# A second head's sums leave their bank by one copy and two transfers

## The chip, the cores and the metric

One core of a Trainium2 chip runs the whole program. The metric is device time in microseconds (us) for one execution. The kernel before takes 528.98 us (median of 3 runs, 528.67 to 529.69).

## The reference, cut to what matters

Three stages follow each other: attention with rotary embedding (2 batches, 8 heads, 576 tokens, 64 wide), a dense feed-forward layer with softplus (1152 tokens, 512 to 2048 to 512), and a mixture of 8 experts of which each token takes one. The change lies in the first stage:

```python
q_rot, k_rot = (rotate(q), rotate(k))
scores = scale * np.matmul(q_rot, k_rot.transpose(0, 1, 3, 2))
scores = scores - np.max(scores, axis=-1, keepdims=True)
attn = np.exp(scores)
attn = attn / (np.sum(attn, axis=-1, keepdims=True) + 1e-09)
attn_out = np.matmul(attn, v)
x = attn_out.transpose(0, 2, 1, 3).reshape(B * S, H * D)
x = x @ w_in            # feed-forward, softplus, w_out, then the experts
```

## The kernel before, in words

Precision is kept by splitting numbers into a high and a low part and adding two or three matmuls, so nearly each PSUM bank is read twice: ScalarE copies the high part (`acopy`, L71), VectorE subtracts it from the bank to get the low part (`vsub`, L74).

**Pairs and slots.** The 16 heads are worked on as 8 pairs (pair 0 to 3 of batch 0, 4 to 7 of batch 1). One loop of slots (the loop over `s`) sets the order of the work on all engines by hand: 9 slots to a pair, 72 in all, and 17 more that mix the last pairs with the feed-forward layer. A slot of pair m computes one 128-row block of scores (`scores`, L526 on TensorE), its maximum (L543 on VectorE) and, in the next slot, its exponentials (L544 on ScalarE). Between these stand the transposes of an earlier pair's exponentials (`turn`, L314) and their products with v (`av`, L612). What is put off to a later slot goes through `later(n, f)`: f is called at the end of the n-th slot from now, and things of one slot in the order in which they were put in.

**The bank of sums.** `av` adds the products of one head of a pair in bank 7 of PSUM (`acc`, 128 rows x 512 tokens). Half of the rows hold the high part of v's product, the other half the low part: head 0 has its high part in rows 0 to 63, head 1 in rows 64 to 127. When a head is through, `fin(m, h)` takes the bank away, and the next head's first `av` (L612, stationary tile from `g`) can only write bank 7 after that. Head 0 of a pair is done at slot 8, head 1 at slot 3 of a period, one and two periods after the pair's own scores.

**Where the sums go.** `xp` (a ring of two buffers, part of the tile the trace calls `g`) is to hold the high parts of both heads, `x_sw` (one buffer, part of the tile `fa`) the low parts, in the same rows as the high ones. So rows have to change halves. Head 0: one copy of all 128 rows into `xp`, and a DMA from `xp`'s lower half to `x_sw`'s upper half (L674). Head 1: two copies by ScalarE of 64 rows each, one to `xp`, one with a change of rows to `x_sw` (L676 and L677, both through L71). Then `finish(m)` on GpSimd (POOL) adds `x_sw` (L691), multiplies by the reciprocals (L687) and splits into the feed-forward layer's input (L68, L81), one step to a slot, from the second slot after on. The last pair (m = 7) goes another way on VectorE.

**What else stands on these queues.** SP issues nearly all DMAs, in program order. In each period it brings the next pair's keys and queries to their places: `kqt` duplicates halves (L335), inserts the last tokens' keys (L350 to L355), brings the low part of the queries (L365), and `load` fetches raw inputs (L233). A score block of the next pair waits for L335 and L365. POOL does the rotary embedding of the pair after next (`rotary`, L264, four steps over four slots), low parts of v (L81), the spreading of reciprocals (L68) and `finish`.

**Scratch.** `y_tl[b]` (128 x 512, part of tile `g`) gathers the last 64 tokens of batch b over its four pairs (`av_tails`), and `x_tails(b)` transposes it after them (slot 65 for batch 0).

Of the kernel before, what the change touches and what calls it, by code (L numbers as in the profile page):

```python
# [20 lines left out]
def kernel(  # L21
# [15 lines left out]
    nc = tc.nc  # L37
# [6 lines left out]
    NP = H // 2  # L44
# [9 lines left out]
    NPR = NH // 2  # L54
# [15 lines left out]
    def acopy(o, i):  # L70
        nc.scalar.activation(out=o, in_=i, func=ACTF.Copy)  # L71
# [116 lines left out]
    y_tl = [vm.take(512), r_tmp.bufs[0]]  # L188
    x_sw = xm[:, 4608:5120]
# [10 lines left out]
    def later(n, fn, start=False):  # L200

        queue.setdefault((now[0] + n, start), []).append(fn)
# [458 lines left out]
    def fin(m, h):  # L661

        r, o = slice(64 * h, 64 * h + 64), slice(64 - 64 * h, 128 - 64 * h)
        if h == 0:
            xps[m] = r_xp.next()
        xp = xps[m]
        acc = pp[:, 7, :]
        if m == NPR - 1:
            tmp = r_tmp.next()
            acopy(tmp[r], acc[o])  # L670
            return lambda: nc.vector.tensor_tensor(out=xp[r], in0=acc[r], in1=tmp[r], op=ALU.add)
        if h == 0:
            acopy(xp, acc)
            nc.sync.dma_start(out=x_sw[r], in_=xp[o])  # L674
        else:
            acopy(xp[r], acc[r])  # L676
            acopy(x_sw[r], acc[o])  # L677
        return None

    def finish(m):  # L680
        b, p = divmod(m, NP)
        last = m == NPR - 1
        eng = nc.vector if last else nc.gpsimd
        xp = xps[m]
        xh, xl = (xt[b][a][:, p, 0:512] for a in range(2))
        steps = [
            lambda: eng.tensor_tensor(out=xp, in0=xp, in1=rsb[m], op=ALU.mult),  # L687
            lambda: (acopy if last else pcopy)(xh, xp),
            lambda: (vsub if last else psub)(xl, xp, xh.bitcast(F32)),
        ]  # L690
        return steps if last else [lambda: eng.tensor_tensor(out=xp, in0=xp, in1=x_sw, op=ALU.add)] + steps  # L691
# [680 lines left out]
    for s in range(NSL + 17):  # L1372
        m, i = divmod(s, 9)
        ma = m - 1 if 4 <= i <= 8 else m - 2
# [7 lines left out]
        if ending:  # L1382
            add = fin(ma, i == 3)
# [29 lines left out]
            add()  # L1413
        if ending and i == 3:
            for n, f in enumerate(finish(ma)):
                later(n + 2, f)
        if extra:
            extra[1]()

# [423 lines left out]
```

## Time and profile before

| | before |
|---|---|
| median of the runs | 528.98 us |
| profiled execution | 529.54 us |
| its span, first to last instruction | 527.8 us |
| TensorE busy in the span | 502.5 us (95%) |
| ScalarE busy | 313.5 us (59%) |
| GpSimd busy | 286.3 us (54%) |
| granted TensorE clock, mean | 0.994 |

The attention's slots lie between about 20 and 190 us of the span; ScalarE, VectorE and GpSimd are much busier there than in the rest. A row of the timeline gives the start and the length of a run of like instructions, and in brackets the idle time of its engine just before it with the name of what ended it. PE rows are matmuls, PEld rows the loading of their stationary tiles, SPq rows the issuing of DMAs (how long SP is held by it, not the transfer).

### The profile page before, as it was taken

Reading aid. Unit: us, or ns where it says so; the run is one execution under the profiler, and the core shown is the slowest. Engines: PE = TensorE matmul, PEld = TensorE weight load, DVE = VectorE, ACT = ScalarE, POOL = GpSimd, SP = SyncE. Lnnn points to the kernel's source line nnn. Section 1 sums busy time; section 2 is a strip of 40 time slices with the busy share of each in tenths; the row PEclk is TensorE's granted clock in tenths of the full one; section 3 lists DMA queues with packets and bytes.
Section 4 is the critical chain, followed back from the end, with each engine's and each line's share of the span. In section 5 each row is a group of like instructions: output and inputs, shape, how many; then the busy total and the mean of one; then the engine's idle time right before and its main releaser. Section 6 shows DMA issues by size and latency. Waiting matters only on the chain. (4 is left out here: it accounts for less than half of the span.)

```text
span 527.8 us, 9308 instructions
## 1 busy us (share of the span) xinstructions
PE 502.5 (95%) x3184; PEld 448.0 (85%) x3184; DVE 351.4 (67%) x766; ACT 313.5 (59%) x662; POOL 286.3 (54%) x308
## 2 busy tenths in 40 slices
PE   8688999999989999999999999999999999999995
PEld 7577888889878999999998788888888989898794
DVE  7867887878899789999898222367656347156220
ACT  5578898999987666655976333345443255345321
POOL 1698889688435655655448655466775535300001
PEclk9989999999999999999999999999999999999998
DMA  7156646545562334544430000522221467500000
GB/s 175 41 136 168 160 120 154 155 115 129 118 185 66 107 120 127 158 149 146 148 122 2 20 22 21 156 67 80 70 95 43 144 264 257 199 9 21 20 6 34
DMA packets 45096, 57.09 MB, mean 108 GB/s; under 512 B 17112, under 2 KB 31448, under 8 KB 45040
## 3 DMA queue, kind: packets, MB, share of 16 engines
q1 hardware_dynamic: 41904, 48.76, 32.4%
q0 software_dynamic: 2704, 7.25, 4.1%
q8 instruction: 27, 0.44, 0.4%
q10 hardware_dynamic: 432, 0.41, 0.2%
q14 instruction: 29, 0.24, 0.2%
HBM read 40.17 MB, written 5.16 MB: 86 GB/s over the span
## 5 line engine op out<-in xcount | busy, mean ns | idle before, releaser
L845 PE MATMUL pp<-rm,parts 128*128 128x512 f32 x432 | 105.5, 397 | 0.4 <-POOL parts L81 0.4
L803 PE MATMUL pp<-xb,rm 128*128 128x288 f32 x768 | 104.4, 295 | 1.1 <-DVE g L820 0.8
L803 PEld LDWEIGHTS pp<-xb,rm 128*128 128x128 f32 x768 | 102.0, 188 | 1.9 <-issue 1.0
L845 PEld LDWEIGHTS pp<-rm,parts 128*128 128x128 f32 x432 | 79.2, 188 | 16.6 <-POOL parts L81 0.9
L314 PE MATMUL pp<-ct,g 128*128 128x128 f32 x388 | 59.0, 274 | 4.3 <-ACT g L71 1.3
L74 DVE TENSOR_TENSOR rm<-pp,rm 128x512 fp32r<-128x512 f32 (+3 forms) x79 | 52.5, 669 | 15.2 <-ACT rm L71 13.8
L544 ACT ACTIVATE g<-pp,negm 128x576 f32<-128x576 f32 x72 | 53.3, 740 | 7.9 <-DVE negm L543 7.5
L314 PEld LDWEIGHTS pp<-ct,g 128*128 128x128 f32 x388 | 46.8, 140 | 13.0 <-DVE rm L74 2.0
L543 DVE TENSOR_REDUCE negm<-pp 128x1 f32<-128x576 f32 x72 | 54.0, 749 | 5.5 <-PE pp L526 5.5
L526 PE MATMUL pp<-rm 128*128 128x288 f32 x216 | 47.6, 329 | 6.3 <-DMA rm<-rm 2.8
L81 POOL TENSOR_TENSOR rm<-fa,rm 128x512 fp32r<-128x512 f32 x34 | 46.3, 1362 | 13.3 <-ACT rm L71 11.0
L1079 PE MATMUL pp<-wa,parts 128*128 128x512 f32 x216 | 51.1, 392 | 0.0
L71 ACT ACTIVATE rm<-pp 128x512 fp32r<-128x512 f32 (+3 forms) x73 | 42.2, 582 | 12.2 <-PE pp L314 7.8
L68 POOL TENSOR_SCALAR rm<-fa 128x512 fp32r<-128x512 f32 x27 | 17.9, 664 | 56.2 <-DVE fa L731 51.4
L1079 PEld LDWEIGHTS pp<-wa,parts 128*128 128x128 f32 x216 | 39.9, 188 | 7.9
L1222 PE MATMUL pp<-wa,wa 128*128 128x256 f32 x320 | 46.3, 283 | 0.0
L81 POOL TENSOR_TENSOR parts<-g,parts 128x512 fp32r<-128x512 f32 (+1 forms) x30 | 36.2, 1224 | 16.7 <-ACT parts L71 16.6
L1222 PEld LDWEIGHTS pp<-wa,wa 128*128 128x128 f32 x320 | 43.0, 192 | 0.2
L526 PEld LDWEIGHTS pp<-rm 128*128 128x128 f32 x216 | 32.5, 194 | 11.8 <-ACT g L544 6.6
L612 PE MATMUL pp<-rm,rm 128*128 128x512 f32 x128 | 41.0, 413 | 0.0
L728 DVE SCALAR_TENSOR_TENSOR fa<-fa 128x512 int32<-128x512 int32 x32 | 40.5, 1265 | 0.8
L264 POOL TENSOR_TENSOR fa<-fa,g 128x512 f32<-128x512 f32 (+1 forms) x30 | 37.2, 1257 | 2.9 <-DMA fa<-in_q_dram 2.0
(219 smaller groups left out, 907.0 us busy)
## 6 DMA issues: line engine op xcount, KB each, us to landing
fa<-in_moe_w_in_dram SPq DMA_DIRECT2D x16, 512.0 KB, 3.9
fa<-in_moe_w_out_dram SPq DMA_DIRECT2D x16, 512.0 KB, 3.5
fa<-in_moe_w_dram SPq DMA_DIRECT2D x16, 512.0 KB, 6.1
rm<-rm SPq DMA_DIRECT2D x56, 128.0 KB, 2.4
ydram<-yst SPq DMA_DIRECT2D x9, 264.0 KB, 2.1
fa<-in_k_dram SPq DMA_DIRECT2D x8, 256.0 KB, 2.9
yst<-in_v_dram SPq DMA_DIRECT2D x8, 256.0 KB, 3.4
st<-in_moe_w_dram POOLq DMA_DIRECT2D x4, 512.0 KB, 8.0
```

What stands on the lines that cost most here:

```text
L71: nc.scalar.activation(out=o, in_=i, func=ACTF.Copy)
L74: nc.vector.tensor_tensor(out=o, in0=a, in1=b, op=ALU.subtract)
L81: nc.gpsimd.tensor_tensor(out=o, in0=a, in1=b, op=ALU.subtract)
L314: nc.tensor.matmul(out=bank[0:a.shape[1], i * 128:(i + 1) * 128], lhsT=a, rhs=ident, is_transpose=True, start=True, stop=True,)
L526: nc.tensor.matmul(out=ps[:, o:o + HS], lhsT=st, rhs=mv[:, k0 + o:k0 + o + HS], start=(x == 0), stop=(x == len(terms) - 1),)
L543: nc.vector.tensor_reduce(out=negm[:, col:col + 1], in_=ps, axis=AX.X, op=ALU.max, negate=True)
L544: return lambda: nc.scalar.activation(out=pr, in_=ps, func=ACTF.Exp, bias=negm[:, col:col + 1], accum_out=sums[:, col:col + 1])
L612: nc.tensor.matmul(out=pp[:, 7, :], lhsT=w, rhs=mv, start=(j == 0 and n == 0), stop=(j == 3 and n == len(terms) - 1))
L803: nc.tensor.matmul(out=hp[:, f, :], lhsT=wv[:, c * 128:(c + 1) * 128], rhs=xt[b][xi][:, c, f * HS:(f + 1) * HS], start=(n_mm == 0), stop=( ...
L845: nc.tensor.matmul(out=ybank(t), lhsT=ghl[gi][:, qd, c, :], rhs=wo[4 * qd + c][wi], start=(qd == 0 and c == 0 and gi == 0 and wi == 0), st ...
L1079: nc.tensor.matmul(out=pp[:, bank, :], lhsT=hid[a][i], rhs=wl[1][i], start=(i == 0 and a == 0 and wl is W.hi), stop=(i == K2F - 1 and a == 1),
L1222: nc.tensor.matmul(out=hp, lhsT=wl[0][2 * c + i // 4][:, i % 4 * 128:i % 4 * 128 + 128], rhs=mem[xi][c], start=(c == 0 and xi == "hi" and ...
```

## The change

For head 1 of pairs 0, 1, 2, 3, 5 and 6, ScalarE no longer makes two copies of 64 rows; it makes one copy of all 128 rows into `both`, which is the `y_tl` of the batch that does not need it at that time, and SP issues two transfers of 64 x 512 numbers, one to `x_sw` and one to `xp`. Pair 4 keeps its two copies (both `y_tl` are in use then), and pair 7 is not touched. The steps of `finish` start one slot later for all pairs but the last.

```diff
         if h == 0:
             acopy(xp, acc)
             nc.sync.dma_start(out=x_sw[r], in_=xp[o])
-        else:
+        elif m == NP:
             acopy(xp[r], acc[r])
             acopy(x_sw[r], acc[o])
+        else:
+
+            both = y_tl[0 if m > NP else 1]
+            acopy(both, acc)
+            nc.sync.dma_start(out=x_sw[r], in_=both[o])
+            nc.sync.dma_start(out=xp[r], in_=both[r])
         return None
...
         if ending and i == 3:
             for n, f in enumerate(finish(ma)):
-                later(n + 2, f)
+                later(n + (2 if ma == NPR - 1 else 3), f)
```

On SP, in the period in which pair 1's second head ends, this stood before (`rm` are the tiles of keys and queries, `fa` holds raw inputs, rotated inputs and `x_sw`, `g_92` holds `xp`):

```order
L355 DMA rm<-rm 128x64
L335 DMA rm<-rm 64x512 x2
L233 DMA fa<-in_q_dram 128x2x256
L335 DMA rm<-rm 64x512 x4
L365 DMA rm<-fa 64x512 x2
L389 DMA rm<-rm 64x4x64 x4
L674 DMA fa<-g_92 64x512
```

and this stands now (`g_92` holds `both` and `xp`):

```order
L355 DMA rm<-rm 128x64
L335 DMA rm<-rm 64x512 x2
L682 DMA fa<-g_92 64x512
L683 DMA g_92<-g_92 64x512
L233 DMA fa<-in_q_dram 128x2x256
L335 DMA rm<-rm 64x512 x4
L365 DMA rm<-fa 64x512 x2
L389 DMA rm<-rm 64x4x64 x4
L674 DMA fa<-g_92 64x512
```

The two new transfers stand between the keys' transfers and the queries' transfers of the pair after; the same holds in the periods of pairs 0, 2 and 3.

On POOL, in the same period, from the spreading of reciprocals on (`rc`), this stood before (`rm_89` is v, `xb_85` and `xb_86` the feed-forward input's high and low part):

```order
L68 TENSOR_SCALAR g_92<-rc 128x512
L264 TENSOR_TENSOR fa<-fa,g_92 128x512
L691 TENSOR_TENSOR g_92<-g_92,fa 128x512
L264 TENSOR_TENSOR fa<-fa,g_92 128x512
L687 TENSOR_TENSOR g_92<-g_92,fa 128x512
L264 TENSOR_TENSOR fa<-fa 128x2x4x32
L81 TENSOR_TENSOR rm_89<-yst,rm_89 128x4x64
L68 TENSOR_SCALAR g_92<-g_92 128x64
L68 TENSOR_SCALAR xb_85<-g_92 128x512
L264 TENSOR_TENSOR fa<-fa 128x2x4x32
L81 TENSOR_TENSOR rm_89<-yst,rm_89 128x4x64
L81 TENSOR_TENSOR xb_86<-g_92,xb_85 128x512
```

and this stands now (the addition is L697 there, the multiplication L693):

```order
L68 TENSOR_SCALAR g_92<-rc 128x512
L264 TENSOR_TENSOR fa<-fa,g_92 128x512 x2
L697 TENSOR_TENSOR g_92<-g_92,fa 128x512
L264 TENSOR_TENSOR fa<-fa 128x2x4x32
L81 TENSOR_TENSOR rm_89<-yst,rm_89 128x4x64
L68 TENSOR_SCALAR g_92<-g_92 128x64
L693 TENSOR_TENSOR g_92<-g_92,fa 128x512
L264 TENSOR_TENSOR fa<-fa 128x2x4x32
L81 TENSOR_TENSOR rm_89<-yst,rm_89 128x4x64
L68 TENSOR_SCALAR xb_85<-g_92 128x512
L264 TENSOR_TENSOR fa<-fa,g_92 128x512
L81 TENSOR_TENSOR xb_86<-g_92,xb_85 128x512
```

The addition moved behind the second step of the rotation, and the last split behind the first step of the next rotation; the amount of work is the same.

## Rows read from the trace of the kernel before

**Rows 1.** The page: busy us, share of the span, instructions.
```profile
PE 502.5 (95%) x3184; PEld 448.0 (85%) x3184; DVE 351.4 (67%) x766; ACT 313.5 (59%) x662; POOL 286.3 (54%) x308
```

**Rows 2.** Waits, 55 to 180 us: who waited for whom, total, times, longest.
```profile
PEld pp L612 <- ACT fa L71: 2.9, 5, 0.7
...
PE pp L612 <- ACT fa L71: 2.3, 6, 0.5
```

**Rows 3.** Timeline of ACT, 59 to 70 us: start, length, engine, line, tiles, shape.
```profile
59.40 0.59 ACT L71 ACTIVATE g<-pp 64x512 f32<-64x512 f32 x1
60.01 0.59 ACT L71 ACTIVATE fa<-pp 64x512 f32<-64x512 f32 x1
...
69.35 0.60 ACT L71 ACTIVATE g<-pp 128x512 f32<-128x512 f32 x1
```

**Rows 4.** Timeline of PE, 60 to 108 us; in brackets the idle time.
```profile
60.65 0.73 PE L612 MATMUL pp<-g 128*128 128x512 f32 x2 [0.43 <-ACT fa L71]
...
70.31 0.43 PE L526 MATMUL pp<-rm,xd 128*128 128x288 f32 x2
...
89.96 0.53 PE L526 MATMUL pp<-rm 128*128 128x288 f32 x2 [0.47 <-DMA rm<-fa]
...
100.48 0.60 PE L314 MATMUL pp<-ct,fa 128*128 128x128 f32 x4
...
107.98 0.43 PE L526 MATMUL pp<-rm,xd 128*128 128x288 f32 x2
```

**Rows 5.** Timeline of SP's issuing, 55 to 125 us.
```profile
63.10 0.58 SPq L233 DMA_DIRECT2D fa<-in_q_dram  x1
64.22 2.51 SPq L335 DMA_DIRECT2D rm<-rm  x4
66.83 1.18 SPq L365 DMA_DIRECT2D xd<-fa  x2
...
74.20 1.28 SPq L386 DMA_DIRECT2D rm<-rm  x2
...
81.52 2.25 SPq L335 DMA_DIRECT2D rm<-rm  x2
83.81 0.59 SPq L233 DMA_DIRECT2D fa<-in_q_dram  x1
84.49 2.99 SPq L335 DMA_DIRECT2D rm<-rm  x4
87.58 1.18 SPq L365 DMA_DIRECT2D rm<-fa  x2
...
91.53 0.55 SPq L674 DMA_DIRECT2D fa<-g  x1
...
100.74 0.58 SPq L233 DMA_DIRECT2D fa<-in_q_dram  x1
101.90 3.08 SPq L335 DMA_DIRECT2D rm<-rm  x4
105.08 1.19 SPq L365 DMA_DIRECT2D xd<-fa  x2
...
118.64 0.58 SPq L233 DMA_DIRECT2D fa<-in_q_dram  x1
120.36 2.38 SPq L335 DMA_DIRECT2D rm<-rm  x4
```

**Rows 6.** DMA issues: tiles, queue, count, KB each, median us to landing.
```profile
fa<-g SPq DMA_DIRECT2D x7, 128.0 KB, 4.4
rm<-fa SPq DMA_DIRECT2D x6, 128.0 KB, 2.3
```

**Rows 7.** Timeline of PEld, 150 to 156 us.
```profile
155.62 0.30 PEld L526 LDWEIGHTS pp<-rm 128*128 128x128 f32 x2 [0.31 <-ACT g L544]
```

**Rows 8.** Timeline of POOL, 79 to 92 us.
```profile
79.40 1.29 POOL L691 TENSOR_TENSOR g<-g,fa 128x512 f32<-128x512 f32 x1 [1.54 <-ACT fa L71]
...
90.78 1.44 POOL L264 TENSOR_TENSOR fa<-fa 128x256 f32<-128x256 f32 x2
```

## The prediction

> **What bounds the kernel now.** I read the busy line of the page first. TensorE is busy for 502.5 of the 527.8 us of the span [rows 1], so only something that removes or adds idle time on TensorE can move the end; ScalarE, at 59%, matters only where TensorE waits for it. So the second view is that of the waits over the attention's slots. It names the line that this change touches: TensorE's products with v (L612) wait for ScalarE's copy to `fa`, which is the second head's copy to `x_sw`. By TensorE's matmul rows this is 2.3 us over six of the seven copies, by the rows of the weight loads 2.9 us over five [rows 2]. The two count the same waits from different ends: the end of a matmul is modelled, the load of the next stationary tile is not hidden after a wait. Third, the timelines show why. ScalarE makes the two 64-row copies one after the other, 0.59 us each; the second ends at 60.60, and TensorE's next head starts at 60.65 after 0.43 us of idle time [rows 3, 4]. Fourth, I read SP's timeline in the same stretches, since that is the queue on which the change puts something.
>
> **What it removes.** A 128-row copy takes 0.60 us, as the first heads' copies show, and a 64-row copy 0.59 [rows 3]: what a copy takes hangs on its columns, not on its rows. So one copy in place of two frees the bank and ScalarE 0.6 us earlier, six times, and the first five of the six waits go. (The sixth of the waits in the view is pair 4's, which is left as it is; pair 6's copy has none.) The mean wait is 2.3 / 6 = 0.38 by the matmuls and 2.9 / 5 = 0.58 by the loads [rows 2]. I take 0.5, so five of them are 2.5 us, with 1.9 and 2.9 as ends. ScalarE being 0.6 us ahead also helps the exponentials just behind; the one place where the next score block visibly waits for them is in pair 5's period, 0.31 us [rows 7], and I take 0.3 for it. Together 2.8 us gained, if nothing is given back.
>
> **What it adds.** Twelve transfers of 128 KB, two in each of six periods. The issue of one holds SP for 0.55 us (L674, same shape), two of the next larger sort for 1.18 (L365) [rows 5]: I take 1.2 us for a pair of them. The ends are 1.1 (two at 0.55) and 2.25 (the dearest pair in these rows, L335 at 81.52) [rows 5]. From issue to landing a lone 128 KB transfer of this form needs 2.3 us, and one from `g` to `fa` had a median of 4.4 [rows 6].
>
> The price hangs on what stands behind them on SP: the raw queries' load, the duplication of the next pair's queries (L335) and their low parts (L365), for which the next pair's first score block waits. I follow TensorE's lead over the kernel before through the periods (minus is earlier).
> - Pair 0. The copy gives -0.5. SP is done with the load at 63.68 and had to wait until 64.22 for ScalarE, so 0.54 of the 1.2 us are free and L365 goes from 66.83 to 67.5 [rows 5]. It lands 2.3 later at 69.8 [rows 6]. The score block that reads it started at 70.31 [rows 4] and would now start at 69.8: just in time, but four transfers more or less at once may be slower. I take 0.2 as lost: -0.3.
> - Pair 1. The copy gives another -0.5. But here SP issues without a pause from 74.20, where it is released by ScalarE, to the end of L365 at 88.76, and TensorE already waits 0.47 us for this very transfer at 89.96 [rows 4, 5]. SP's chain starts 0.3 earlier and is 1.2 longer: L365 at 88.5, landed at 90.8. TensorE stands at +0.85. What two copies gave is gone, and more.
> - Pair 2. -0.5 makes +0.35. SP's run begins with ScalarE's work and so 0.85 later; its pause of 0.58 before 101.90 is used up: L365 goes from 105.08 to 106.6 and lands at 108.9, where TensorE read it at 107.98 [rows 4, 5]. +0.9.
> - Pair 3. -0.5 makes +0.4. SP has 1.14 us of pause between the load (ends 119.22) and the duplication at 120.36 [rows 5], enough for the two issues, and no wait for a transfer stands in TensorE's rows there. +0.4.
> - Pair 5. -0.5 and the 0.3 from above make -0.4. No queries are moved any more. Pair 6: no wait before, none after.
>
> So about 2.4 of the 2.8 us are given back and -0.4 is left. Against its own execution (529.54: span 527.8, 1.74 around it) that is 529.1; against the median of the runs, which is 0.56 lower, **528.6 us**.
>
> The Trainium skill speaks against my largest term. The page "DMA: Bandwidth & Descriptors", section "Issuing engines are not separate DMA queues", says that the sequencer time it takes to start a DMA is usually small beside the DMA itself. By that rule two more issues would not count, and the result would be that of the second case below. The rows differ from it here: 0.59 us of issue stand against 2.3 to landing, but SP issues without a pause from 74.20 to 88.76 [rows 5], and at 89.96 it is the end of this row of issues that TensorE waits for.
>
> **The later finish on POOL.** The addition waited 1.54 us for ScalarE's copy [rows 8]. Now it waits for two transfers. In pair 1's period these are issued from about 83.5 on and land by 86.6, so POOL, in order, stands for some 7 us instead, with two steps of one rotation and all of the next behind it. That next rotation ended at 92.2 [rows 8] and would end near 98; its reader, TensorE's transposes of the rotated inputs, comes at 100.48 [rows 4]. I cost this at nothing, with these 2 to 3 us as its cover. If the transfers need 4.4 us instead of 2.3, the cover falls below 1 us.
>
> **The rivals.**
> - *Hidden issues (the full gain).* SP's 1.2 us are swallowed, for instance because its long issues (0.75 mean in the four at 84.49, 1.1 in the two at 81.52 [rows 5]) are pauses that would happen anyway and overlap. For it: SP does pause in pairs 0, 2 and 3. Against it: the 0.47 at 89.96. Time: 528.98 - 2.8 = 526.2, with 1.9 alone 527.1; I say 526.6.
> - *POOL held by the transfers (slower).* The addition stands in order before the rotations. From a landing of about 5 us after the issue on, the transposes at 100.48 and their like in the next two periods wait. L674's median of 4.4 [rows 6] speaks for it; that it is issued just ahead of larger loads, as the new ones are too, explains it. With a landing of 5.5 to 6.5 us TensorE waits about 1 us in each of three periods beside the forecast's -0.4: 528.98 - 0.4 + 3 x 0.9 = 531.3; with two of three 530.4.
> - *Dear issues (slower or same).* A pair of issues takes the upper end, 2.25. Then pairs 1 and 2 end 1 us later each, against which pair 3's pause gives some back: +1.0 on top of the forecast, 529.6.
> - *The bank is not what holds L612.* Then TensorE waits at the same place for the exponentials and only the 1.2 us on SP remain: about 529.5. Against it: start at 60.65, 50 ns after the copy's end.
>
> **How the numbers follow.** Forecast 0.45 (own range 527.9 to 529.6), hidden issues 0.32, POOL held 0.13, dear issues 0.06, another holder of the bank 0.04. A measurement of this kernel can tell about 0.2%, 1.1 us, from no change, so faster means under 527.9 and slower over 530.0. Faster: 0.29 of the second case, 0.05 of the first, 0.34. Slower: 0.12 from POOL, 0.02 each from the last two, 0.04 from the forecast's upper tail, 0.20. The rest, 0.46, is the same. The range for 8 times in 10 is 526.4 to 530.4: from nearly all of the gain to POOL held in two of three periods.
>
> **What would show it.** Right: in the profile after, L612's waits for ScalarE's copy shrink to pair 4's one; SP's rows show the two issues between L335 and the load, about 1.2 us; the wait of TensorE for `rm` from `fa` (0.47 at 89.96) grows to 1.5 to 2.5 us at the first block of pair 4, and a smaller one appears at the block of pair 5. POOL's addition waits for a DMA and no longer for ScalarE, without anyone waiting for POOL's rotations. Wrong: no wait for L335 or L365 grows (then it is the full gain), L314 waits for POOL's L264 (then the slower rival), or L612 waits at the same place for something else.

## The result and the profile after

The changed kernel takes **534.42 us** (median of 6 runs, 533.19 to 539.89), the kernel before in the same session 529.12 (6 runs, 527.74 to 530.58). The ratio is 1.0116, 95% interval 1.007 to 1.0161: slower, where 528.6 with a range up to 530.4 was forecast. The profiled execution took 534.74, with a span of 533.1 and a granted clock of 0.996; that of before had 529.54, 527.8 and 0.994. Between 58 and 131 us the granted clock is 1.00 in both, so the clock is not where the 5.3 us of span went.

The busy line of the page after answers to [rows 1]:

```profile
PE 502.7 (94%) x3184; PEld 448.2 (84%) x3184; DVE 355.9 (67%) x766; ACT 308.0 (58%) x656; POOL 286.5 (54%) x308
```

TensorE is busy as long as before (502.7 against 502.5), so the whole loss is idle time. ScalarE lost six instructions and 5.5 us of work, and VectorE gained 4.5 us of busy time with the same 766 instructions. Of these 4.5 us, 4.1 are in the first step of the reciprocals (L550), whose 16 instructions have a mean of 435 ns instead of 181: five of them lie beside operations of GpSimd here, one of these (at 37.93 us) before anything of the change has run. Some 3 us behind each of the other four, TensorE's transposes wait for VectorE (L314 for L74): 1.6 us in four waits, where it was 0.7 in one.

The view of waits, 55 to 190 us, TensorE's matmul rows (who waited for whom, total, times, longest), answers to [rows 2]:

```profile
PE pp L526 <- DMA rm<-rm: 3.0, 2, 1.9
PE pp L526 <- ACT g L544: 2.0, 3, 1.4
...
PE pp L612 <- DVE rm L74: 0.7, 2, 0.4
PE pp L526 <- DMA xd<-fa: 0.7, 2, 0.4
PE pp L612 <- ACT fa L71: 0.4, 1, 0.4
PE pp L612 <- POOL g L81: 0.3, 1, 0.3
```

The wait that the change aims at went from 2.3 us in six to 0.4 in one, pair 4's, as forecast. In its place stands L526, the score block that opens the next pair: 3.0 us for `rm` from `rm`. That is L335, the duplication of the queries; L365, on which the prediction counted, ends a second, shorter wait of the same blocks. Two waits for VectorE (L612 <- DVE) were in nobody's sum.

Two rows of the timeline before that are needed for the comparison:

```profile
59.43 0.79 PE L526 MATMUL pp<-rm 128*128 128x288 f32 x4
...
126.04 0.78 PE L526 MATMUL pp<-rm 128*128 128x288 f32 x4
```

TensorE's timeline after, first the row ahead of the first copy, then those that answer to [rows 4]:

```profile
60.05 0.80 PE L526 MATMUL pp<-rm 128*128 128x288 f32 x4
60.68 0.62 PE L612 MATMUL pp<-g 128*128 128x512 f32 x2
...
71.06 0.50 PE L526 MATMUL pp<-rm 128*128 128x288 f32 x2 [1.09 <-DMA rm<-rm]
71.91 0.54 PE L526 MATMUL pp<-rm,xd 128*128 128x288 f32 x2 [0.35 <-DMA xd<-fa]
...
92.18 0.50 PE L526 MATMUL pp<-rm 128*128 128x288 f32 x2 [1.90 <-DMA rm<-rm]
92.87 0.54 PE L526 MATMUL pp<-rm 128*128 128x288 f32 x2 [0.19 <-DMA rm<-fa]
...
111.33 0.50 PE L526 MATMUL pp<-rm 128*128 128x288 f32 x2 [1.35 <-ACT g L544]
112.18 0.54 PE L526 MATMUL pp<-rm,xd 128*128 128x288 f32 x2 [0.36 <-DMA xd<-fa]
...
130.64 1.16 PE L526 MATMUL pp<-rm 128*128 128x288 f32 x4 [0.32 <-issue]
```

The block at 60.05 stood at 59.43 in the kernel before, so this execution came 0.62 late out of the start, before anything of the change had run. I take that off. The first product after the copy (60.68 against 60.65 before) has no wait any more and is 0.6 us early. Then the lead turns round: +1.0 at 71.91, +2.3 at 92.87, +3.6 at 112.18, against -0.3, +0.85 and +0.9 in the prediction. (The row at 111.33 names ScalarE as the last to release it: exponentials that run from 110.50 to 111.23. The same ones of pair 0's period run from 70.50 to 71.23, and the block there starts at 71.06, before their end. So the block does not need them, and L335 is left, whose issues end at 109.3; 2.9 us to landing, the median below, fit.)

SP's issuing in pairs 0, 1 and 2 (start, length, line, tiles, count) answers to [rows 5]:

```profile
62.48 2.10 SPq L335 DMA_DIRECT2D rm<-rm  x2
64.67 0.55 SPq L682 DMA_DIRECT2D fa<-g  x1
65.27 0.59 SPq L683 DMA_DIRECT2D g<-g  x1
65.91 0.58 SPq L233 DMA_DIRECT2D fa<-in_q_dram  x1
66.59 2.40 SPq L335 DMA_DIRECT2D rm<-rm  x4
69.09 1.18 SPq L365 DMA_DIRECT2D xd<-fa  x2
...
85.14 1.77 SPq L683 DMA_DIRECT2D g<-g  x1
...
87.64 2.38 SPq L335 DMA_DIRECT2D rm<-rm  x4
90.12 1.19 SPq L365 DMA_DIRECT2D rm<-fa  x2
...
104.94 1.89 SPq L233 DMA_DIRECT2D fa<-in_q_dram  x1
106.92 2.38 SPq L335 DMA_DIRECT2D rm<-rm  x4
109.40 1.18 SPq L365 DMA_DIRECT2D xd<-fa  x2
```

An issue is 0.55 to 0.6 us, as taken, but in each of these periods one issue of the row ahead of the queries' four L335 is far longer: 1.77 at 85.14 and 1.89 at 104.94, and the pair at 62.48 takes 2.10 instead of some 1.2. The pauses of 0.54 and 0.58 us in [rows 5], which the prediction spent on the new issues, are gone: SP issues in one row from 62.48 to the end of L365. The duplications also take longer on their way than before. The table of issues (count, KB each, median us to landing), which answers to [rows 6], has

```profile
rm<-rm SPq DMA_DIRECT2D x56, 128.0 KB, 2.9
...
fa<-g SPq DMA_DIRECT2D x13, 128.0 KB, 3.6
...
rm<-fa SPq DMA_DIRECT2D x6, 128.0 KB, 2.4
g<-g SPq DMA_DIRECT2D x6, 128.0 KB, 3.7
```

The first of these had a median of 2.4 before. That is not what the new transfers do to it in general: with two idle transfers in the same places, in a run below, it is 2.4 and 4.2 us are lost all the same. The prediction took 2.3 us to landing for what gates the block. From the start of L365 to the block that reads it, it is 2.8 us here: from 69.09 to 71.91, from 90.12 to 92.87, from 109.40 to 112.18.

GpSimd's addition, in answer to [rows 8], in pair 1's period:

```profile
88.93 1.28 POOL L697 TENSOR_TENSOR g<-g,fa 128x512 f32<-128x512 f32 x1 [6.68 <-ACT rm L71]
```

It stands for 6.7 us, about the 7 forecast. (The row names ScalarE; but the transfer of 85.14, with 3.7 us to landing, comes in at 88.8, just ahead of the addition.) TensorE waits for GpSimd 0.3 us in all: the slower rival did not come about.

### The profile page after: what moved, and what is told of

Read it like the earlier page. It is cut to its first block, busy times and chain, and to the rows that moved or that the text cites. A ratio compares the mean times of both kernels' runs of the same rounds, so it can differ in the third digit from the quotient of the medians.

```text
span 533.1 us, 9329 instructions
## 1 busy us (share of the span) xinstructions
PE 502.7 (94%) x3184; PEld 448.2 (84%) x3184; DVE 355.9 (67%) x766; ACT 308.0 (58%) x656; POOL 286.5 (54%) x308
## 5 line engine op out<-in xcount | busy, mean ns | idle before, releaser
L314 PE MATMUL pp<-ct,g 128*128 128x128 f32 x388 | 59.7, 275 | 6.1 <-DVE rm L74 2.5
L74 DVE TENSOR_TENSOR rm<-pp,rm 128x512 fp32r<-128x512 f32 (+3 forms) x79 | 52.4, 669 | 17.0 <-ACT rm L71 16.0
L314 PEld LDWEIGHTS pp<-ct,g 128*128 128x128 f32 x388 | 46.8, 140 | 15.3 <-DVE rm L74 4.0
L526 PE MATMUL pp<-rm 128*128 128x288 f32 x216 | 47.3, 326 | 9.3 <-DMA rm<-rm 5.1
L81 POOL TENSOR_TENSOR rm<-fa,rm 128x512 fp32r<-128x512 f32 x34 | 46.3, 1361 | 13.3 <-ACT rm L71 11.0
L81 POOL TENSOR_TENSOR parts<-g,parts 128x512 fp32r<-128x512 f32 (+1 forms) x30 | 36.2, 1224 | 16.9 <-ACT parts L71 16.9
L526 PEld LDWEIGHTS pp<-rm 128*128 128x128 f32 x216 | 32.2, 192 | 14.3 <-ACT g L544 4.9
L612 PE MATMUL pp<-rm,rm 128*128 128x512 f32 x128 | 41.6, 415 | 0.7 <-DVE rm L74 0.7
L264 POOL TENSOR_TENSOR fa<-fa,g 128x512 f32<-128x512 f32 (+1 forms) x30 | 37.3, 1257 | 3.4 <-DMA fa<-in_q_dram 3.0
```

Source lines behind the costliest of these rows:

```text
L74: nc.vector.tensor_tensor(out=o, in0=a, in1=b, op=ALU.subtract)
L81: nc.gpsimd.tensor_tensor(out=o, in0=a, in1=b, op=ALU.subtract)
L314: nc.tensor.matmul(out=bank[0:a.shape[1], i * 128:(i + 1) * 128], lhsT=a, rhs=ident, is_transpose=True, start=True, stop=True,)
L526: nc.tensor.matmul(out=ps[:, o:o + HS], lhsT=st, rhs=mv[:, k0 + o:k0 + o + HS], start=(x == 0), stop=(x == len(terms) - 1),)
L612: nc.tensor.matmul(out=pp[:, 7, :], lhsT=w, rhs=mv, start=(j == 0 and n == 0), stop=(j == 3 and n == len(terms) - 1))
```

## The experiments

All are timed beside the kernel before, whose medians lay between 528.75 and 528.94. Line numbers of a kernel shift by some lines with its edits; the tiles tell which instruction it is.

**Is it the transfers, and what of them?**

*The change without its transfers.* Both `dma_start` of the change removed; the rows they fill are cleared once on GpSimd (so the second heads' sums are left out of the output).

```diff
             acopy(both, acc)
-            nc.sync.dma_start(out=x_sw[r], in_=both[o])
-            nc.sync.dma_start(out=xp[r], in_=both[r])
```

> The change with both transfers left out: one copy of 128 rows to the scratch tile, nothing is brought to x_sw and xp, so the second heads' sums are not in the output (x_sw and xp's lower rows are cleared once on POOL instead). It gives what the copy alone is worth. Theory A (SP's issue time of the two transfers delays the queries' transfers), theory B (their bytes slow the landings of the transfers beside them) and theory C (POOL's addition, waiting in order for the transfers, holds the rotations) all expect the full gain here: 2 to 3 us under the kernel before, about 526.5 us, with the waits of L612 for the copy gone except pair 4's. If the copy is worth less than the prediction's 2.8 us, it shows here: then 528 to 529.

Measured: 529.59, ratio 1.0006 (0.9987 to 1.0025). So the transfers are nearly all of the loss; but the copy and the later finish together gain nothing that this interval shows, where 2 to 3 us were expected by all three theories. The second question below starts here.

*Small transfers.* The two transfers move 16 of the 512 columns (the rest of those rows is left out and cleared once on GpSimd).

```diff
-            nc.sync.dma_start(out=x_sw[r], in_=both[o])
-            nc.sync.dma_start(out=xp[r], in_=both[r])
+            nc.sync.dma_start(out=x_sw[r, 0:16], in_=both[o, 0:16])
+            nc.sync.dma_start(out=xp[r, 0:16], in_=both[r, 0:16])
```

> The change with both transfers cut to 16 of 512 columns: the same number of issues on SP at the same places, a 32nd of the bytes (the other columns of the second heads' sums are missing from the output). Theory A: the issues cost the same, so about the time of the change, 533 to 535 us, and TensorE waits at the first block of pairs 3, 4 and 5 for L335 or L365 for 1 to 2 us as in the change. Theory B: the bytes are gone, so about 527 us and these waits fall to those of the kernel before (0 to 0.5). Half way, about 530, would mean that both count.

Measured: 535.04, ratio 1.0118 (1.0083 to 1.0153), as the change itself. The bytes cost nothing that shows, and TensorE waits as long for `rm` from `rm` as with the full transfers (3.5 us against 3.0). (After the longest of these waits, 2.19 us at 91.30, the granted clock of this execution is 0.62 from 92 to 96 us, where the lower of the two levels, 1.2 of 2.4 GHz, would be 0.5; after the change's wait of 1.90 us it stayed at 1.00.) SP's rows read 0.55 and 0.59 us for these transfers at 63.85 and 64.45, the same as with 128 KB.

*The kernel before with two idle transfers.* The same number, size and place of issues, with data that nobody reads, and nothing else.

```diff
             acopy(x_sw[r], acc[o])
+            if m != NP:
+                idle = y_tl[0 if m > NP else 1]
+                table = rpt.rearrange("p a w -> p (a w)")
+                nc.sync.dma_start(out=idle[r], in_=table[o, 0:512])
+                nc.sync.dma_start(out=idle[o], in_=table[r, 0:512])
```

> The kernel before, its two copies and its order of finish unchanged, with two more transfers of 64 x 512 numbers on SP at the places where the change has them (from the rotation's table to a scratch tile that is free then; nobody reads them). It gives the price of the transfers alone. Theories A and B: the change is 5.3 us slower although the copy should give 2 to 2.8, so the price is 7 to 8 us: 536 to 537 us, with waits for L335 or L365 at the first blocks of pairs 3, 4 and 5. Theory C: POOL does not wait for these transfers, so 529 to 530 us.

Measured: 533.56, ratio 1.008 (1.0051 to 1.011), 4.2 us by the ratio: less than the 7 to 8 expected. The score blocks wait as after the change, where the kernel before had 0.5 us for one of these lines. Its waits, in the same view:

```profile
PE pp L526 <- DMA rm<-rm: 1.0, 1, 1.0
...
PE pp L526 <- DMA xd<-fa: 0.8, 2, 0.6
...
PE pp L526 <- issue: 0.6, 1, 0.6
PE pp L526 <- DMA rm<-fa: 0.6, 2, 0.4
```

*The same two idle transfers, issued behind L335 and L365.*

```diff
-                nc.sync.dma_start(out=idle[r], in_=table[o, 0:512])
-                nc.sync.dma_start(out=idle[o], in_=table[r, 0:512])
+                later(2, lambda: nc.sync.dma_start(out=idle[r], in_=table[o, 0:512]))
+                later(2, lambda: nc.sync.dma_start(out=idle[o], in_=table[r, 0:512]))
```

> The kernel before, with the same two idle 128 KB transfers a pair as in the run that cost 4.7 us, but issued at the end of slot 5, behind the duplications L335 and L365 instead of ahead of them. Theory A (place in SP's row): nearly the whole price goes, 528.8 to 529.8, and the blocks near 70, 89, 108 and 126 us wait no longer than before. Theory B (the transfers cost by what they take of the DMA engines, wherever they stand): 532 to 534.

Measured: 529.08, ratio 1.0011 (0.9996 to 1.0026). The same work on the same queue, two slots later, costs 0.1% instead of 0.8%. None of the four waits above is left in its view. This settles theory A: the price of a transfer here is its place in SP's row. What the price is made of is not settled. With the idle transfers ahead, each of the four periods has an issue that is far longer than its like (85.54: 1.47 for the load; 122.78: 2.14 for the second transfer; the four L335 at 65.75 and 105.05 take 3.49 and 3.89 instead of 2.4). With the transfers behind, the four L335 take 2.6 to 3.0 and no other issue is long. No run parts the two issues' own time from that of the long ones.

*The change with the raw queries' load behind L335 and L365.*

```diff
-        if i == 4 and m and m + 2 < NPR:
+        if i == 5 and m and m + 2 < NPR:
             load(m + 2, "xq")
```

> The change, with the raw queries' load issued one slot later, so that on SP it stands behind the duplications of the queries (L335) and of the tails (L365) instead of ahead of them. Theory A (the price is the place in SP's row: what stands ahead of L335 sets when the first score block can go): one load's issue, 0.6 us in the trace of the change and up to 1.9 where it took long, leaves the path in pairs 1, 2 and 3, so the waits ahead of the first blocks at 92, 111 and 131 us shrink by 0.6 to 1.5 each and the time is 531.5 to 533. Theory B (the transfers hold back the landing of the others in the DMA engines, wherever they were issued): the waits stay at 1.9, 1.6 and 0.3, the time is 534 to 535. Against both: the later load makes the rotation of the queries late; then POOL is waited for by the queries' transposes of the next period.

Measured: 531.18, ratio 1.0047 (1.0022 to 1.0072): one issue less ahead of L335, and more than half of the loss is back. What stood against both theories is seen too, once: the products with v wait for GpSimd's low parts of v (L81), which stand in order behind the rotation of the queries.

```profile
PE pp L612 <- POOL g L81: 1.4, 1, 1.4
```

After this wait the granted clock is 0.57 from 116 to 120 us, so part of what is left of the loss in this execution is the clock.

*The change with its transfers on GpSimd's queue.* `nc.gpsimd.dma_start` in both places.

> The change with both transfers issued by POOL's queue instead of SP's, all else equal. Theory A: SP is free of them, L335 and L365 go out as in the kernel before, and the copy's gain stays: 526.5 to 528 us. Theory B: the same bytes move at about the same time, so 532 to 534 us. Theory C: POOL now also spends time on issuing and waits for the landing all the same, so 533 us or more, with TensorE's L314 waiting for POOL's L264.

Measured: ratio 1.009 (1.006 to 1.012), 4.8 us, no gain that the intervals can tell. SP is free of the two issues, but GpSimd's work now lies elsewhere, and TensorE waits for it, straight and through VectorE. The first two rows are waits; the third, of VectorE's timeline, is the first step of the reciprocals, which takes 2.65 us beside two of GpSimd's operations (0.59 at most in the kernel before), and the L74 of the first wait stands behind it:

```profile
PE pp L314 <- DVE g L74: 2.9, 2, 2.0
PE pp L612 <- POOL g L81: 1.8, 1, 1.8
...
77.10 2.65 DVE L550 TENSOR_SCALAR rc<-sums 128x8 f32<-128x8 f32 x1
```

After the longest wait of either kind the granted clock is 0.57 (82 to 86 and 123 to 127 us). So this run does not tell what a free SP alone would have given.

*The change with its transfers behind L365, and the finish four slots after the sums.*

```diff
-            nc.sync.dma_start(out=x_sw[r], in_=both[o])
-            nc.sync.dma_start(out=xp[r], in_=both[r])
+            later(2, lambda: nc.sync.dma_start(out=x_sw[r], in_=both[o]))
+            later(2, lambda: nc.sync.dma_start(out=xp[r], in_=both[r]))
...
-                later(n + (2 if ma == NPR - 1 else 3), f)
+                later(n + (2 if ma == NPR - 1 else 4), f)
```

> The change with both transfers issued at the end of slot 5, behind L335 and L365, and the finish four slots after the sums. Theory A: the first blocks wait as in the kernel before; left are the copy's saving (0.5) and the later finish's price (1.0 with three slots), so 529 to 530. Rival (GpSimd's addition, in order, now stands for the transfers until they land, some 5 us later than in the change, and the rotation behind it is late): 531 to 534 with TensorE waiting for GpSimd.

Measured: 538.48, ratio 1.0196 (1.0171 to 1.022). Here the rival of the prediction that had not come about with the change does: GpSimd's addition stands for the transfer, and TensorE waits for what is behind it in GpSimd's order, the rotation (L264) and the low parts of v (L81). The first row is GpSimd's timeline, the others the waits:

```profile
94.50 1.26 POOL L697 TENSOR_TENSOR g<-g,fa 128x512 f32<-128x512 f32 x1 [8.15 <-DMA g<-g]
```

```profile
PE pp L612 <- POOL g L81: 3.6, 1, 3.6
PE pp L314 <- POOL fa L264: 3.5, 3, 2.4
```

The addition starts at 94.50, where it was 88.93 with the change: the first was inside GpSimd's cover, the second is not. The loss, 10.4 us by the ratio, is not these waits alone. After TensorE's waits of 2.40 us (to 96.50) and 3.65 us (to 123.66) the granted clock is 0.51 from 98 to 101 us and 0.50 from 123.6 to 128, the lower of its two levels (1.2 of 2.4 GHz), and TensorE is busy for 506.0 us in all, against 502.7 with the change.

**Where did the copy's 2.8 us go?**

*The kernel before with the later finish alone.*

```diff
-                later(n + 2, f)
+                later(n + (2 if ma == NPR - 1 else 3), f)
```

> The kernel before, with one edit of the change alone: GpSimd's finish of a pair starts three slots after the sums instead of two (all but the last pair); the copies stay as they were and there is no transfer. Theory F (the later finish costs by itself, between 155 and 175 us, where its four steps come beside VectorE's unpacking of weights, and this is what ate the copy's saving in the run without transfers): 530 to 531, with the loss at 155 to 175 us. Rival G (the place of the finish costs nothing; the loss there comes from the copy or from the arrival of the pair at another time): 528.6 to 529.2.

Measured: 529.83, ratio 1.0019 (1.0003 to 1.0036): 1.0 us (0.2 to 1.9), where the prediction put nothing. VectorE's, GpSimd's and TensorE's timelines of this run:

```profile
162.98 1.51 DVE L724 TENSOR_SCALAR fa<-fa 128x512 int32<-128x512 int32 x1
...
166.22 1.52 DVE L724 TENSOR_SCALAR fa<-fa 128x512 int32<-128x512 int32 x1
```

```profile
162.89 1.31 POOL L687 TENSOR_TENSOR g<-g,fa 128x512 f32<-128x512 f32 x1
...
165.75 1.71 POOL L81 TENSOR_TENSOR xb<-g,xb 128x512 fp32r<-128x512 f32 x1
```

```profile
165.14 0.50 PE L612 MATMUL pp<-rm,rm 128*128 128x512 f32 x1 [0.42 <-DVE rm L74]
168.52 0.50 PE L612 MATMUL pp<-rm,rm 128*128 128x512 f32 x1 [0.34 <-DVE rm L74]
```

L724, the first step of the unpacking of the weights, takes 1.5 us where it overlaps one of GpSimd's operations on two tiles, and ends 0.3 us behind it both times (164.49 after 164.20, 167.74 after 167.46). VectorE's subtraction L74 comes 0.7 to 1.1 us later, and TensorE waits for it. In the kernel before, GpSimd's multiplication was done by 158.6, and the same two instructions took 0.81 and 0.41. The Trainium skill has a rule for it: the page "SBUF — State Buffer", section "SBUF: two separate sides", says that VectorE, in its modes with two ports or with two inputs from SBUF, and GpSimd share a pair of ports, which the one that starts first holds for its whole instruction while the other stands still. These rows agree with that: GpSimd's operation started first both times (162.89 and 165.75) and VectorE's ends just behind its end. In which mode L724 ran, they do not show.

*The later finish for all but pair 5.*

```diff
-                later(n + (2 if ma == NPR - 1 else 3), f)
+                later(n + (2 if ma in (5, NPR - 1) else 3), f)
```

> The kernel before with the finish three slots after the sums for every pair but the fifth (and the last): the finish of pair 5 stays two slots after them. Theory F (the price of the late finish is paid at pair 5, where its multiplication on GpSimd, L687, falls beside VectorE's unpacking L724, which then takes 1.5 us instead of 0.4 to 0.8 and holds up L74, for which the products with v wait): the two waits for VectorE of 0.3 to 0.4 at 165 and 169 us go, and the time is that of the kernel before, 528.6 to 529.1. Rival (the late finish costs in every pair, or through pair 6): the waits or the time of 529.8 stay.

Measured: 528.42, ratio 0.9996 (0.998 to 1.0012). Both waits for VectorE are gone, and its rows are back to the lengths of before:

```profile
162.74 0.81 DVE L724 TENSOR_SCALAR fa<-fa 128x512 int32<-128x512 int32 x1
...
165.84 0.41 DVE L724 TENSOR_SCALAR fa<-fa 128x512 int32<-128x512 int32 x1
```

The price of the later finish is paid in pair 5's period, and the other pairs add nothing that this interval (-1.1 to +0.6 us) shows.

*The change without transfers and with the early finish* (the second heads' sums are left out again).

```diff
-                later(n + (2 if ma == NPR - 1 else 3), f)
+                later(n + 2, f)
```

> The change without its transfers (the rows that they would fill hold zeros, so the odd head's half of the outputs is left out) and with the finish two slots after the sums, as before. Theory F (the later finish ate the copy's saving): 527 to 528, and no loss at 155 to 175 us. Rival G (the finish is indifferent): as with the late finish, 529.6, with the loss at 155 to 175 us kept. Theory D (saved waits are given back at the first score blocks): the steps ahead of them at 70, 89 and 108 us are 0.3 to 0.5 longer than before.

Measured: 528.24, ratio 0.9983 (0.9969 to 0.9998): 0.9 us gained, 0.1 to 1.6. So the copy's saving is real but small, though all five waits for it are gone. TensorE's timeline shows where the rest goes, ahead of the score blocks:

```profile
70.26 0.50 PE L526 MATMUL pp<-rm 128*128 128x288 f32 x2 [0.44 <-DMA xd<-fa]
...
89.65 0.53 PE L526 MATMUL pp<-rm 128*128 128x288 f32 x2 [0.56 <-DMA rm<-fa]
107.35 0.50 PE L526 MATMUL pp<-rm 128*128 128x288 f32 x2 [0.66 <-ACT rm L71]
```

TensorE comes to these blocks earlier and finds them not ready.

*The kernel before with the second 64-row copy on VectorE* (in all pairs but 4 and 7, so in pair 6 as well).

```diff
+        elif m == NP:
+            acopy(xp[r], acc[r])
+            acopy(x_sw[r], acc[o])
         else:
             acopy(xp[r], acc[r])
-            acopy(x_sw[r], acc[o])
+            nc.vector.tensor_copy(x_sw[r], acc[o])
```

> The kernel before, with one edit: in pairs 0, 1, 2, 3 and 5 the second of the two 64-row copies (to x_sw) is made by VectorE beside ScalarE's, so that both halves leave the bank at once and no transfer is issued. Theory C (the copy's saving is real, the price lay on SP): the waits of 0.4 to 0.5 at the sums' next owner go, as they did with the change, nothing is added to SP, the time is 526.5 to 528. Theory D (a saved wait here is given back at the first score block whatever SP does, since the queries' duplications end the wait there, as the run without transfers suggests): 528.5 to 529.5. Theory E (VectorE is late itself at that place, its queue in order): the wait for ScalarE turns into one for VectorE, 529.5 to 531.

Measured: 531.77, ratio 1.0054 (1.0034 to 1.0074), theory E. VectorE's copy takes 0.68 us, TensorE now waits for that, and its waits for the exponentials grow from 1.3 to 3.7 us; the row maxima that the exponentials need stand behind the copy on VectorE:

```profile
PE pp L526 <- ACT g L544: 3.7, 6, 0.7
PE pp L612 <- DVE fa L680: 2.6, 5, 0.7
```

*The kernel before with the load behind L335 and L365* (the edit of the load alone).

> The kernel before, with one edit: the raw queries' load is issued one slot later, behind L335 and L365 on SP. Theory A (what stands ahead of L335 and L365 on SP sets when the next pair's first block can go, in the kernel before too): the 0.47 at 89.96 us goes and the blocks near 70 and 108 us are no earlier, 528.0 to 528.8. Rival (the later load makes GpSimd's rotation of the queries late, as seen in the run of the change with the load behind, where the products with v waited 1.35 us for GpSimd): 529.5 to 531.

Measured: 527.67, ratio 0.9985 (0.9967 to 1.0004). The 0.47 us at the block of [rows 4] at 89.96 is gone, but the interval holds no change as well.

*One copy of the bank, the halves moved by GpSimd, the finish early.*

```diff
-            nc.sync.dma_start(out=x_sw[r], in_=both[o])
-            nc.sync.dma_start(out=xp[r], in_=both[r])
+            moves[m] = lambda: (pcopy(x_sw[r], both[o]), pcopy(xp[r], both[r]))
...
+            if ma in moves:
+                later(2, moves[ma])
             for n, f in enumerate(finish(ma)):
-                later(n + (2 if ma == NPR - 1 else 3), f)
+                later(n + 2, f)
```

> The change with its two transfers replaced by two copies on GpSimd (0.62 us each by the trace of before), two slots after the sums, ahead of the addition, and with the finish two slots after the sums as before. Nothing is added to SP. Theory C (the copy's saving is real, about 0.5 us as in the run without transfers and with the early finish; GpSimd has 1 to 3 us of pause a pair): 528.0 to 528.6, a shade under the kernel before. Rival (1.2 us more on GpSimd, in order, make a rotation late): TensorE waits for GpSimd's rotations, 529.5 to 531.

Measured: **527.11**, ratio 0.9966 (0.9947 to 0.9984), with nothing of the computation left out. GpSimd's pauses took the two copies (0.61 and 0.62 us at 64.50 and 65.20), and the addition follows without a wait.

*The same with the load behind L335 and L365.*

> The run with the two copies on GpSimd in place of the transfers, and with the raw queries' load one slot later, behind L335 and L365 on SP. Theory A (in the kernel without transfers, too, the queries' duplications end the wait at the first blocks, so the copy's saving is kept whole only when they start earlier): the waits of 0.4 us for rm from fa go, 526.0 to 527.0. Rival (the later load makes GpSimd, now 1.2 us a pair fuller, late with the rotation of the queries): TensorE waits for L81 of GpSimd near 117 us, 527.5 to 529.5.

Measured: **526.78**, ratio 0.9955 (0.9939 to 0.9971), the best of all: by the ratio 2.4 us under the kernel before. No wait of TensorE for a DMA or for GpSimd is left in the stretch; what is left is 4.1 us in eight waits for VectorE's and ScalarE's work, pair 4's copy (0.4) among them.

## Why the prediction was wrong

**What it removes: right as a wait, too large as a gain.** L612's waits went as forecast, five of six. But 2.8 us stood under "if nothing is given back", and the giving back was looked for on SP's two new issues alone. Without any new issue 0.9 us (0.1 to 1.6) is left. The first blocks of the next pairs, of which only one showed a wait in [rows 4], had next to no slack: "just in time" was written of pair 0's and was true of three.

**What it adds: the step that failed.** The step is the one that follows the lead through the pairs and gives back 2.4 us in all. Its mechanism is right: the two issues push L335 and L365 back, and TensorE waits for them at the next pair's first block. Its sizes are too small, for one reason on SP and one on the way. On SP one issue in each period is far longer than the others, and the sum had every issue at its usual length. On the way it is 2.8 us from L365's issue to the block, where the forecast took 2.3.
- *Pair 0.* SP's pause of 0.54 us took up part of the two issues, as forecast. But the long issue (2.10 for a pair of L335, 0.9 too much) came on top: L365 was issued at 69.09, which is 1.6 us later than before with the 0.62 taken off, instead of 0.7. From its copy at 60.68 to 71.91 pair 0 lost 1.6 us instead of 0.2.
- *Pair 1* lost 1.3 us, copy's gain included, against the 1.15 forecast (-0.3 to +0.85). The kind is right, the size is partly luck: SP's row grew by 0.9 (L365 at 90.12 is 1.9 late, 1.0 of them brought along) and not by 1.2, since it had held long issues before as well (2.25 for two L335 and 2.99 for four in [rows 5]), and the way was 0.45 longer than taken.
- *Pair 2* lost 1.3 us, copy's gain included, from 92.87 to 112.18, instead of 0.05. Its pause was used up, as forecast. SP's row grew by 1.4 (L365 at 109.40 is 3.7 late, 2.3 of them brought along) instead of 0.6: the long issue is 1.3 us too much, less the 0.7 that the four L335 had taken longer before (3.08 against 2.38).
- *Pair 3* was forecast free, so that the copy's 0.5 us would stay. Its pause of 1.14 us was used up too; one issue took 1.75 us (at 122.97), and TensorE waited. The shift went from +3.6 at 112.18 to +4.0 at the block of 130.64, which stood at 126.04 before; the four matmuls of that block then take 1.16 us instead of 0.78, so that +4.4 stand behind it. That is 0.8 us lost, copy's gain included.

By itself the term is measured with the idle transfers: 4.2 us (2.7 to 5.8) instead of 2.4. That it is place and not bytes was in the prediction and is shown by the two runs with small and with moved transfers. Why there is a long issue is open.

The Trainium skill's page "DMA: Bandwidth & Descriptors", section "Issuing engines are not separate DMA queues", calls the time to start a DMA usually small beside the DMA. As a comparison of lengths the trace agrees (0.55 against 2.4 to 3.7 us to landing). As a statement on cost it misleads here: ahead of L335 these 0.55 us cost 0.8% of the kernel, and behind it 0.1%.

**The later finish: costed at nothing, 1.0 us.** The cover named for it, GpSimd's 2 to 3 us ahead of the rotations' readers, held: 0.3 us of waits for GpSimd. The price lay where I had not looked, in VectorE's lengthened L724 in pair 5's period, 60 us behind the place that I checked.

**The sum.** The three parts by themselves are -0.9, +4.2 and +1.0, together +4.3; the change is at 1.0116, 6.1 us with an interval from 3.7 to 8.5. The parts explain it within that interval; whether 1 to 2 us more come from the parts acting on each other is open.

**The rivals.** Hidden issues, given 0.32, are refuted by the idle transfers: 4.2 us are not hidden. GpSimd held by the transfers is refuted for the change (0.3 us) and shown for a version with later transfers. Dear issues were given 0.06 and a time of 529.6: in kind that is nearest to what happened, one long issue in each period, but in the four periods of pairs 0 to 3 and not in two. That the bank is not what holds L612 is refuted: the waits went with the copy.

## What to carry to other kernels

An issue on a queue can cost next to nothing or much of its length, by what stands behind it: find the next transfer in that queue for which the bound engine waits, and put new work behind it or on an engine with pauses. A wait that goes is worth only the slack of the next wait of the same engine; "no wait is shown there" is not slack, so a gain should be followed to the next two or three points where the engine could stand. And a step moved in time is to be checked against what it then lies beside, at every repetition, not in one period.

## What the runs showed that I had not expected

- In the change, one SP issue in each of the four periods takes 1.5 to 1.9 us instead of 0.55 to 0.6. The kernel before has such issues in pairs 1 and 2 (2.25 for the two L335 at 81.52 in [rows 5]) and none in pairs 0 and 3. They fall on different instructions. A 16 KB packet of a queue that the trace calls an instruction queue starts within 0.2 us of each of the change's four (62.90, 85.24, 104.91, 122.84; of the two L335 at 62.48 the second is the long one). In the kernel before, one at 120.08 falls into SP's pause there, and one at 65.43 beside issues of the usual length. That is a coincidence in time; it was not tried.
- The length of an issue does not hang on its bytes: 0.55 and 0.59 us with 16 columns as with 512.
- A wait of TensorE can cost more than its length: after 3.65 us of it the granted clock was 0.50 for 4.4 us. After other waits of about 2 us it fell in one run (2.19 us, 0.62 behind it) and not in another (1.90 us, 1.00).
- VectorE's operation on one tile of integers takes 0.41 us alone and 1.5 beside GpSimd's operations on two tiles. No wait shows it, the instruction is just longer; L550 is the same case (37.93 to 39.21 us in the change, 1.28 us beside GpSimd's rotation).
- A GpSimd copy from one half of the partitions to the other takes 0.61 us for 64x512, like one within a half (0.62): the two replace two transfers, with their issue and their 3.6 us to landing.
